# Full-width key and query projections, spread to head rows by DMA, in a gated two-attention kernel

## The chip, the cores and the metric

The kernel runs on one core of one Trainium2 chip. The metric is device time in microseconds (us) of one execution. The core has five engines: TensorE (PE, with its weight loads as PEld), VectorE (DVE), ScalarE (ACT), GpSimd (POOL) and SyncE (SP), which here issues nearly all DMAs. Each engine runs its own instructions in program order; the order between engines comes from semaphores.

## The reference, cut to what matters

```python
g = sigmoid((x * gate_w).sum(-1, keepdims=True))          # x: 1 x 2048 x 512, bf16
# A: full softmax attention, 32 heads of 16
qkv = (x @ A_wqkv).reshape(B, S, 3, 32, 16).transpose(2, 0, 3, 1, 4)
p = softmax(einsum("bhqd,bhkd->bhqk", q, k) * 16 ** -0.5)
a = heads_to_columns(einsum("bhqk,bhkd->bhqd", p, v)) @ A_wo
# B: the same shapes, but a query sees only 8 keys: its own row and every second row before it
idx = pos[:, None] - 2 * arange(8)[None, :]               # masked where negative
b = heads_to_columns(windowed_attention(x @ B_wqkv, idx)) @ B_wo
return g * a + (1 - g) * b
```

## The kernel before

**A planner writes the program.** The class `Sched` simulates the five engines while the kernel is built. Every piece of work is an `Op` with an engine, a duration, dependencies, a due time and the buffers it takes and gives back (`Slots`: two general PSUM buffers "m", two PSUM score rings "rA" and "rB" of 3 and 2 banks, one accumulator "acc", and SBUF buffers). The planner picks, engine by engine, the piece that can start soonest and is due first; that order becomes the program order. Its durations and start times are numbers in the code, such as `S_.t["DVE"] = 2500.0` for the time at which VectorE is taken to be free. On the chip only the order remains, with semaphores.

**Attention A.** The 32 heads are handled as 8 groups of 4; the 2048 queries as 4 chunks of 512 (`QW`), the keys as 16 tiles of 128. One group with one query chunk is a period; there are 32 periods. A unit of work is one head, one key tile and one query chunk: a 128 x 512 block of scores. A period has 64 units, the kernel 2048. In `kt_all` each group's 4 heads sit at partitions 0, 32, 64, 96 with 16 rows of keys each; row 16 of each is a row of ones. The query tile `qt` has the same layout with 16 rows of queries, and row 16 holds minus an upper bound of the scores, so that one 32-row matmul gives score minus bound. Each unit's exponential is made in one of two ways:

- on ACT: PE writes 3 or 2 units into a ring, ACT takes exp of the whole ring (`pT<-ring`, 128x1536 or 128x1024), and PE multiplies with the values (`acc<-pT,vp_all`);
- on DVE, in "quads" of 4 units (`make_quad`): four conversions from PSUM (`dt<-m_ps`), two further terms made in SBUF (`dt<-dt`, 128x2048), and 12 matmuls (`acc<-dt,...`). The planner starts a quad when it sees VectorE free (`d_source`, `start_quad`).

**Projections.** `k_proj` makes one group's keys for 512 positions: four zeroing matmuls (`mm_init`, which also write the row of ones), then 16 matmuls of only 16 columns each, one per head and 128-row slice of the input, each in its own 32-column tile of the array; VectorE copies the result into `kt_all` and takes the largest magnitude (`kmax_all`). `selk` builds a small matrix from it. `q_proj` does the same for queries, takes magnitudes (`absq`), multiplies them with that matrix to fold in the bound (`bound`), and copies out `qt`. `v_proj` projects values with 128-column weights. For the first group the keys are copied by ACT (`first=True`). Each next pair of groups is prepared while the present pair's 8 periods run (`hooks`).

**Attention B.** `b_tile` handles 128 rows at a time, 16 tiles. PE projects, the keys and values go through DRAM (`kv_scr`) and come back shifted 8 times (`ksh`, `vsh`). POOL does nearly all arithmetic in order: 8 products with the query, sums (`prod<-prod`) to logits `lg`, then (`lg<-lg,mx`) the subtraction of the maximum; ACT takes the exponential (`lg<-lg`), VectorE the sum; POOL normalises (`lg<-lg,rr`), multiplies 8 values, adds, and writes `obb`. `final` mixes both attentions for 128 rows and writes them out; the last rows need the last `obb`.

**Keeping PE busy.** `zero_pass` inserts matmuls with zero weights where the planner sees PE's recent activity fall.

Of the kernel before, what the change touches and what calls it, by code (L numbers as in the profile page):

```python
# [36 lines left out]
def _mean_log_ratio():  # L37
    n = 4096
    acc = 0.0
    for k in range(n):  # L40
        y = 128.0 * k / n
        s = 0.0
        for o, w in zip(OFFS, WTS):
# [15 lines left out]
          ("ACT", "DVE"): 1000.0, ("DVE", "POOL"): 800.0, ("SP", "POOL"): 1500.0, ("POOL", "ACT"): 1000.0}  # L59
# [58 lines left out]
class Sched:  # L118
# [31 lines left out]
    def pe_run(self, mms, start, state=None, count=False):  # L150
# [5 lines left out]
        for m, tile_, cols in mms:  # L156
            if m != mode:
                if state is None and count:
                    self.switches += 1
                t = max(t, max(busy) + (SWITCH if "r" in (m, mode) else 0.0))  # L160
                mode = m
            ks = range(4) if tile_ is None else (tile_,)
            t = max(t, max(busy[k] for k in ks))
            if first is None:
                first = t
            if count:
                self.streamed.append((t, t + cols / 2.4, 1.0 if tile_ is None else 0.25))
            for k in ks:
                busy[k] = t + cols / 2.4 + 2.5
            last = t + 174.0 + cols / 2.4  # L170
            t += 15.0
# [112 lines left out]
    def warm(self, ready, op):  # L284

        mms = [("f", None, QW)]
# [45 lines left out]
def kernel(  # L332
# [71 lines left out]
    KEPT = 11  # L404
    for name_, n_ in (("m", 2), ("rA", 1), ("rB", 1), ("acc", 1), ("pTA", 3), ("pTB", 3), ("qt", 3), 
                      ("dt", 8), ("accT", 2), ("ott", 2), ("ksv", 2), ("prod", 1), ("lg", 2),
                      ("kvs", 1), ("qb", 1), ("osb", 3), ("keep", KEPT + 16), ("fb", 1)):
        S_.slots[name_] = Slots(n_)
# [15 lines left out]
    e32 = const.tile([128, 32], BF16, name="e32")  # L424
    V.memset(e32[:], 0.0)
    V.memset(e32[0:1, DH:DH + 1], 1.0)
    selq = const.tile([128, 128], BF16, name="selq")
    V.memset(selq[:], 0.0)
    for j in range(4):
        V.memset(selq[32 * j:32 * j + DH, 32 * j + DH:32 * j + DH + 1], 1.0)  # L430
    ident = const.tile([128, 128], BF16, name="ident")
    make_identity(nc, ident[:])

# [9 lines left out]
    kmax_all = const.tile([128, NG, NC], FP32, name="kmax_all")  # L443
    kmax = const.tile([128, NG], FP32, name="kmax")
    selk_all = const.tile([128, NG, 128], BF16, name="selk_all")
# [5 lines left out]
    S_.t["POOL"] = 9000.0  # L451
    S_.t["DVE"] = 2500.0
# [23 lines left out]
    for name, o, lo in (("wk0", wkv[:, :, 0:G1], D), ("wq0", wq[:, :, 0:G1], 0), ("wv0", wkv[:, :, D:D + G1], 2 * D)):  # L476
        with nc.allow_non_contiguous_dma(reason="columns of one head group"):
            A.dma_start(out=o, in_=a_w3[:, :, lo:lo + G1])
        ld[name] = S_.add(Op("SP", lambda: None, dur=1.0, due=-10.0, lat=4500.0, name=f"ld_{name}"))
    load("x0", x_load(0), 8100.0)  # L480
# [37 lines left out]
    kt_ops = {}  # L518

    def k_proj(i, sc, due, first=False):  # L520
        hold = Hold("m")
        st = {}

        def part(c0, c1):
            def s():
                if c0 == 0:
                    st["pk"] = misc_ps(hold, [128, QW])
                    mm_init(st["pk"], e32, QW)
                pk = st["pk"]
                for c in range(c0, c1):  # L530
                    for j in range(4):
                        h = 4 * i + j
                        mm(pk[32 * j:32 * j + DH, :], wkv[:, c, h * DH:(h + 1) * DH],
                           xT[:, c, sc * QW:(sc + 1) * QW], False, c == DC - 1, tile_position=(0, 32 * j))
            return s

        def evac():
            o = kt_all[:, i, sc * QW:(sc + 1) * QW]
            if first:
                A.copy(out=o, in_=st["pk"][:])  # L540
            else:
                V.tensor_copy(out=o, in_=st["pk"][:])

        def red():
            src = st["pk"][:] if first else kt_all[:, i, sc * QW:(sc + 1) * QW]
            V.tensor_reduce(out=kmax_all[:, i, sc:sc + 1], in_=src, axis=AX.X, op=ALU.max, apply_absolute_value=True)
        slow = 2 if first and sc == 0 else 1
        p1 = Op("PE", part(0, 2), mms=COL4 * (3 * slow), deps=xt_ops[sc] + [ld["wk0" if i == 0 else "wk"]], due=due, acq=[hold], not_before=0.0 if first else due - 5000.0,
                name="k1")
        p2 = Op("PE", part(2, DC), mms=COL4 * (2 * slow), deps=[p1], due=due, name="k2")  # L550
        for o in (p1, p2):
            S_.add(o)
        if first:
            r = S_.add(Op("DVE", red, dur=700.0, deps=[p2], due=due, name="kred"))
            e = S_.add(Op("ACT", evac, dur=650.0, deps=[p2, r], due=due, rel=[hold], name="kev"))
        else:
            e = S_.add(Op("DVE", evac, dur=683.0, deps=[p2], allow=400.0, rel=[hold], name="kev"))
            r = S_.add(Op("DVE", red, dur=677.0, deps=[e], allow=1500.0, name="kred"))
        kt_ops.setdefault(i, []).append(e)
        return r  # L560

    selk_ops = {}

    def selk(i, reds, due):
        def s():
            V.tensor_reduce(out=kmax[:, i:i + 1], in_=kmax_all[:, i, :], axis=AX.X, op=ALU.max)
            V.tensor_scalar(out=selk_all[:, i, :], in0=selq[:], scalar1=kmax[:, i:i + 1], scalar2=-1.02,
                            op0=ALU.mult, op1=ALU.mult)
        selk_ops[i] = S_.add(Op("DVE", s, dur=446.0, deps=reds, due=due, lock=True, name="selk"))
# [3 lines left out]
    def v_proj(h0, h1, tb, TB, due):  # L573
# [4 lines left out]
        def mk(half):  # L578
            def s():
# [3 lines left out]
                for tt in range(lo, hi):  # L583
                    t = tb + tt
                    for c in range(DC):
                        mm(st["pv"][:, tt, :], xT[:, c, t * 128:(t + 1) * 128],
                           wkv[:, c, D + h0 * DH:D + h1 * DH], c == 0, c == DC - 1)
            return s

        def evac():  # L590
# [3 lines left out]
        ops = [Op("PE", mk(0), mms=[("f", None, max(n, 140))] * per, due=due, acq=[hold], not_before=due - 5000.0 if h0 else 0.0,  # L594
                  begun=[] if h0 else [qb_ops[(0, 0)]], name="v1")]
        if TB > 1:
            ops.append(Op("PE", mk(1), mms=[("f", None, max(n, 140))] * per, due=due, name="v2"))
# [19 lines left out]
    qt_ops, qb_ops = {}, {}  # L617

    def q_proj(c_, i, due):
        hold, hq, ha = Hold("m" if (c_, i) != (0, 0) else "acc"), Hold("qt"), Hold("accT")  # L620
        st = {}

        def part(c0, c1):
            def s():
                if c0 == 0:
                    st["p1"] = misc_ps(hold, [128, QW]) if hold.res == "m" else ps.tile([128, QW], FP32, tag="acc", bufs=1, name="p1")
                    mm_init(st["p1"], z32, QW)
                for c in range(c0, c1):
                    for j in range(4):
                        h = 4 * i + j  # L630
                        mm(st["p1"][32 * j:32 * j + DH, :], wq[:, c, h * DH:(h + 1) * DH],
                           xT[:, c, c_ * QW:(c_ + 1) * QW], False, c == DC - 1, tile_position=(0, 32 * j))
            return s

        def absq():
            a = sb(ha, [128, QW], I32, "absq")
            V.tensor_scalar(out=a[:], in0=st["p1"][:].bitcast(I32), scalar1=0x7FFFFFFF, scalar2=None, op0=ALU.bitwise_and)
            st["absq"] = a

        def bound():  # L640
            hi = st["absq"][:].bitcast(BF16).rearrange("p (n two) -> p n two", two=2)[:, :, 1]
            mm_ct(st["p1"], selk_all[:, i, :], hi, False, True, skip_group_check=True)

        def evac():
            qt = sb(hq, [128, QW], BF16, "qt")
            V.tensor_copy(out=qt[:], in_=st["p1"][:])
            qt_tiles[(c_, i)] = qt
        ops = [Op("PE", part(0, 2), mms=COL4 * 3, deps=xt_ops[c_] + [ld["wq0" if i == 0 else "wq"]], due=due, acq=[hold, hq, ha], begun=selk_ops[i].deps if (c_, i) != (0, 0) else [],
                  name="q1"),
               Op("PE", part(2, DC), mms=COL4 * 2, due=due, name="q2"),  # L650
               Op("DVE", absq, dur=683.0, allow=300.0, name="qabs"),
               Op("PE", bound, mms=COL4, due=due, rel=[ha], deps=[selk_ops[i]], name="qb"),
               Op("DVE", evac, dur=683.0, allow=300.0, rel=[hold], name="qev")]
        S_.chain(ops)
        qt_ops[(c_, i)] = (ops[-1], hq)
        qb_ops[(c_, i)] = ops[3]
# [4 lines left out]
    def g_jobs(due):  # L661
# [3 lines left out]
        def zmm():  # L665
            st["zp"] = misc_ps(hz, [128, NT])
            for t in range(NT):
                for c in range(DC):
                    mm(st["zp"][:, t:t + 1], xT[:, c, t * 128:(t + 1) * 128], gw[:, c:c + 1], c == 0, c == DC - 1)
# [5 lines left out]
        def zfin():  # L675
# [4 lines left out]
        ops = [Op("PE", zmm, mms=[("f", None, 70)] * 64, due=due, deps=[o for v in xt_ops.values() for o in v] + [ld["gw"]],  # L680
                  acq=[hz], name="z"),
# [492 lines left out]
    def emit_fill(us, res, n, op):  # L1174
        ring = ps.tile([128, n, QW], FP32, tag=res, bufs=1, name="ring")
        for _ in range(op.zeros):
            mm(ring[:, 0, :], zw[:], ones_t[:], True, True)
# [132 lines left out]
    def make_quad(p, t, late):  # L1310
# [7 lines left out]
        for j in range(4):  # L1318
# [3 lines left out]
            def fill(j=j, hold=hold, st=st):  # L1322
                f_ = fops[j]
                st["s"] = misc_ps(hold, [128, QW])
                for _ in range(f_.zeros):
                    mm(st["s"][:], zw[:], ones_t[:], True, True)
# [151 lines left out]
```

## Time and profile before

| what | value |
|---|---|
| time, median of 3 runs | 800.84 us (797.55 to 804.08) |
| the profiled execution's own time | 798.02 us |
| its span, first to last instruction | 796.0 us |
| busy: PE / DVE / ACT / POOL | 738.2 / 676.4 / 756.2 / 695.4 us |
| mean granted TensorE clock | 0.992 |
| exponentials on ACT: 3-unit / 2-unit, mean | x329, 1530 ns / x328, 1103 ns |
| first exponential of attention A begins | 18.47 us |
| first product of attention B on POOL begins | 56.70 us |
| last `obb` on POOL begins | 787.31 us, lasts 1.27 us |

The span is the stretch between the first and last instruction; about 2 us of the execution lie outside it. Nearly every instruction is recorded at one helper line (L382), so rows are told apart by their tiles: `pT<-ring` reads tile `ring` and writes `pT`. A busy engine need not be the bound: what counts is what its successors wait for.

### The profile page before, as it was taken

The page shows a single profiled execution, that of the slowest core. Times are in us where ns is not written, and L with a number is a line of the kernel's source. Part 1 is how long each engine was busy: PE and PEld are TensorE (multiplying, and loading weights), DVE is VectorE, ACT ScalarE, POOL GpSimd, SP SyncE. Part 2 cuts the span into 40 slices and gives each one's busy share as a digit, 9 for nine tenths or more (in the row PEclk, how much of TensorE's full clock was granted, in tenths as well). Part 3 has the DMA queues.
Part 4 walks back from the last instruction along what each step waited for, and adds up shares of the span by engine and source line. Part 5 has one row for each costly group of instructions (what it writes and reads, how often), then busy time and mean ns, then how long its engine had stood idle before and what let it go on. Part 6 is the DMA issues. An engine that isn't in the chain of part 4 may idle for free.

```text
span 796.0 us, 20219 instructions
## 1 busy us (share of the span) xinstructions
PE 738.2 (93%) x8481; PEld 237.4 (30%) x8481; DVE 676.4 (85%) x1013; ACT 756.2 (95%) x680; POOL 695.4 (87%) x599
## 2 busy tenths in 40 slices
PE   7999999999999989999989899999999989999996
PEld 2332222333232223333322222333222222222222
DVE  3369899888989998989997888978998898888985
ACT  2899999899999999999999999999999999999993
POOL 1019799999999999999899999999998999999896
PEclk9799999999999999999999999999999999999999
DMA  9220321032011212111111121101122210122100
GB/s 206 88 68 12 109 67 55 18 104 68 22 47 54 68 54 68 55 50 42 45 68 54 54 67 54 65 18 55 56 67 81 68 54 30 53 68 67 61 15 34
DMA packets 52074, 47.46 MB, mean 60 GB/s; under 512 B 12048, under 2 KB 49424, under 8 KB 51984
## 3 DMA queue, kind: packets, MB, share of 16 engines
q1 hardware_dynamic: 50400, 45.98, 18.6%
q8 instruction: 66, 1.08, 0.6%
q10 hardware_dynamic: 1584, 0.20, 0.2%
q14 instruction: 24, 0.20, 0.1%
HBM read 37.75 MB, written 6.32 MB: 55 GB/s over the span
## 4 chain that ended last, share of the span: by engine, by line
ACT 29%; PE 28%; DVE 16%; POOL 16%; issue 9%; SPq 1%; DMA 0%; POOLq 0%; DVEq 0%; ACTq 0%
ACT pT L382 29%; POOL prod L382 13%; PE m_ps L382 13%; DVE dt L382 11%; PE acc L382 8%; PE ring L382 7%; SPq L382 1%; POOL lg L382 1%; DVE accT L382 1%; POOL obb L382 1%; POOL ott L382 0%; DVE kt_all L382 0%; DMA xT<-in_A_x_dram 0%; DVE kvs L382 0%; DVE vd_all L382 0%
## 5 line engine op out<-in xcount | busy, mean ns | idle before, releaser
L382 ACT ACTIVATE pT<-ring 128x1536 bf16<-128x1536 f32 (+1 forms) x658 | 750.1, 1316 | 13.2 <-PE ring L382 11.8
L382 PE MATMUL ring<-qt,kt_all 32*128 32x512 bf16 x1644 | 278.0, 383 | 31.0 <-ACT pT L382 25.3
L382 POOL TENSOR_TENSOR prod<-prod 128x512 f32<-128x512 f32 x224 | 295.2, 1324 | 10.8
L382 DVE TENSOR_SCALAR dt<-m_ps 128x512 uint16<-128x512 f32 x404 | 265.3, 676 | 26.8 <-PE m_ps L382 17.5
L382 DVE TENSOR_SCALAR dt<-dt 128x2048 uint16<-128x2048 uint16 x202 | 224.5, 1116 | 1.6 <-PE acc L382 1.0
L382 PEld LDWEIGHTS <-kt_all 32*128 32x128 bf16 (+1 forms) x2304 | 98.1, 91 | 293.1 <-issue 280.8
L382 POOL TENSOR_TENSOR prod<-ksh,qb 128x512 f32<-128x512 bf16 x128 | 161.7, 1292 | 5.6 <-DMA ksh<-kv_scr 3.3
L382 PE MATMUL acc<-pT,vp_all 128*17 128x512 bf16 x1644 | 158.1, 384 | 0.0
L382 POOL TENSOR_TENSOR prod<-vsh,lg 128x512 f32<-128x512 bf16 x128 | 152.2, 1208 | 3.5
L382 PE MATMUL m_ps<-qt,kt_all 32*128 32x512 bf16 x404 | 135.6, 381 | 5.8 <-DVE dt L382 4.5
L382 POOL TENSOR_TENSOR ott<-accT,rden 128x256 bf16<-128x256 f32 x31 | 25.0, 807 | 60.9 <-DVE rden L382 60.8
L382 PEld LDWEIGHTS <-vp_all 128*17 128x17 bf16 x2048 | 46.0, 88 | 107.4 <-issue 99.2
L382 PE MATMUL acc<-dt,vd_all 128*17 128x512 bf16 x808 | 61.1, 379 | 0.0
L382 PE MATMUL m_ps<-bw,xT 128*32 128x512 bf16 x768 | 55.6, 382 | 3.2 <-DVE dt L382 2.0
L382 PE MATMUL acc<-ones_t,zw 128*32 128x512 bf16 (+1 forms) x235 | 51.2, 391 | 1.3 <-DVE accT L382 1.2
L382 PEld LDWEIGHTS <-xT 128*32 128x32 bf16 (+1 forms) x1152 | 32.5, 97 | 32.9 <-issue 26.5
L382 PE MATMUL acc<-dt,vp_all 128*17 128x512 bf16 x404 | 39.6, 383 | 0.0
L382 PE MATMUL m_ps<-xT,wkv 128*16 128x512 bf16 x512 | 38.3, 388 | 1.2 <-DMA xT<-in_A_x_dram 1.2
L382 PE MATMUL m_ps<-xT,wq 128*16 128x512 bf16 x496 | 36.0, 380 | 0.0
L382 DVE TENSOR_SCALAR absq<-m_ps 128x512 int32<-128x512 int32 x31 | 21.3, 686 | 14.7 <-PE m_ps L382 14.4
L382 DVE CAST kt_all<-m_ps 128x512 bf16<-128x512 f32 x28 | 19.2, 687 | 13.3 <-PE m_ps L382 13.0
L382 PEld LDWEIGHTS <-zw 128*32 128x32 bf16 (+1 forms) x367 | 16.7, 94 | 42.7 <-issue 40.8
(72 smaller groups left out, 450.5 us busy)
## 6 DMA issues: line engine op xcount, KB each, us to landing
ksh<-kv_scr SPq DMA_DIRECT2D x16, 1024.0 KB, 5.5
vsh<-kv_scr SPq DMA_DIRECT2D x16, 1024.0 KB, 5.5
kv_scr<-kvs SPq DMA_DIRECT2D x16, 256.0 KB, 2.0
out_dram<-osb SPq DMA_DIRECT2D x16, 128.0 KB, 1.7
bw<-in_B_wqkv_dram SPq DMA_DIRECT2D x1, 1536.0 KB, 9.9
wkv<-in_A_wqkv_dram SPq DMA_DIRECT2D x2, 448.0 KB, 4.9
bwo<-in_B_wo_dram SPq DMA_DIRECT2D x1, 512.0 KB, 3.7
woarr<-in_A_wo_dram SPq DMA_DIRECT2D x8, 64.0 KB, 2.2
```

Of the source, the lines that this page charges most:

```text
L382: return chain_on(key, f(*a, **k))
```

## The change

Keys and queries are projected for two groups (eight heads) at once. `pair_proj` runs four 32-column tiles over the 128 columns of eight heads, without zeroing matmuls. `pair_k` copies the 128x512 result to a buffer `kr`, takes its largest magnitudes, and 8 DMAs of 16x512 spread it into the head rows of `kt_all`. `pair_q` copies to `qr`, makes the magnitudes there and scales them by minus the bound (`kbnd`), sends queries and bound rows to a DRAM tile (`scr`) with two DMAs and fetches each group's query tile with one more. The bound now occupies 16 rows beside each head's 16 query rows, and 16 rows of ones in `kt_all` face them. These ones are written once, at the start, by 7 memsets on VectorE for groups 1 to 7. Group 0 is done differently (`k_first`, `q_first`): VectorE first writes each head's columns of the weights twice side by side (`dup`, into `wd0`), the projection then fills all 32 rows, and small per-row factors (`isq`, `isk`, `isb`, `sgn`, made from the identity matrix) turn the second half into ones or bounds. `selk`, `absq` and the bound's matmuls are gone. The value projection and the zero passes use four 32-column tiles instead of one full-width matmul. The planner's tables are adapted: the buffers (`qt` 4 instead of 3, new `kr` 2 and `qr` 1, `KEPT` 8 instead of 11), margins for SP, a charge for every change of array mode, and the time at which VectorE is taken to be free at the start.

```diff
-    KEPT = 11
+    KEPT = 8
...
-                t = max(t, max(busy) + (SWITCH if "r" in (m, mode) else 0.0))
+                t = max(t, max(busy) + SWITCH)
...
+    r16 = ident[:].rearrange("p (a two d) -> p two a d", two=2, d=DH)
+    V.tensor_reduce(out=isq[:], in_=r16[:, 0], axis=AX.XY, op=ALU.max)
...
     G.memset(vp_all[:, :, :, DH:DH + 1], 1.0)
-    S_.t["POOL"] = 9000.0
-    S_.t["DVE"] = 2500.0
+    for g in range(1, NG):
+        V.memset(kt_all[:, g, :], 1.0)
+    S_.t["DVE"] = 7000.0
...
+    def dup(k, src):
+        for two in range(2):
+            V.tensor_copy(out=wd0[:, k, :, :, two, :], in_=src[:, :, 0:G1].rearrange("p c (h d) -> p c h d", d=DH))
+    for k, name, src in ((0, "wk0", wkv), (1, "wq0", wq)):
+        ld[name + "d"] = S_.add(Op("DVE", lambda k=k, src=src: dup(k, src), dur=420.0, deps=[ld[name]], due=-10.0, lock=True, name="dup"))
...
+    def heads_proj(out, k, sc, c0, c1):
+        for c in range(c0, c1):
+            for j in range(4):
+                mm(out[32 * j:32 * j + 32, :], wd0[:, k, c, j].rearrange("p two d -> p (two d)"), xT[:, c, sc * QW:(sc + 1) * QW],
+                   c == 0, c == DC - 1, tile_position=(0, 32 * j))
...
+    def pair_proj(w2, m, sc, due, hold, acq, deps, name):
...
+                for c in range(c0, c1):
+                    mm_ct(st["p"], w2[:, c, 128 * m:128 * m + 128], xT[:, c, sc * QW:(sc + 1) * QW], c == 0, c == DC - 1)
...
+    def pair_k(w2, m, n, dues, dst, deps, acq, name, groups=(0, 1)):
...
+            def spread(sc=sc, st=st):
+                for e in groups:
                     for j in range(4):
+                        SP.dma_start(out=dst(e)[32 * j:32 * j + DH, sc * QW:(sc + 1) * QW], in_=st["r"][64 * e + DH * j:64 * e + DH * j + DH, :])
...
+    def pair_q(w2, m, sc, n, due, deps, acq, tiles, name, groups=(0, 1)):
...
+            st["r"] = sb(hr, [128, 2, QW], BF16, "qr")
+            V.tensor_copy(out=st["r"][:, 0, :], in_=st["p"][:])
+        def mag():
+            q_, a_ = st["r"][:, 0, :].bitcast(I32), st["r"][:, 1, :].bitcast(I32)
+            V.tensor_scalar(out=a_, in0=q_, scalar1=0x7FFF7FFF, scalar2=None, op0=ALU.bitwise_and)
+            V.tensor_scalar(out=st["r"][:, 1, :], in0=st["r"][:, 1, :], scalar1=kbnd[:, n:n + 1], scalar2=None, op0=ALU.mult)
+        def put():
+            for two in range(2):
+                r = scr[0, 16 * two:16 * two + 1, :]
+                SP.dma_start(out=_ap(r, [[32 * QW, 8], [QW, DH], [1, QW]]), in_=st["r"][:, two, :])
+        def get():
+            for h, e in zip(acq, groups):
+                t_ = sb(h, [128, QW], BF16, h.res)
+                SP.dma_start(out=t_[:], in_=scr[e])
...
     def v_proj(h0, h1, tb, TB, due):
...
-                        mm(st["pv"][:, tt, :], xT[:, c, t * 128:(t + 1) * 128],
-                           wkv[:, c, D + h0 * DH:D + h1 * DH], c == 0, c == DC - 1)
+                        mm_ct(st["pv"][:, tt, :], xT[:, c, t * 128:(t + 1) * 128],
+                              wkv[:, c, D + h0 * DH:D + h1 * DH], c == 0, c == DC - 1)
...
     def zero_pass(now):
...
-        mm(acc_tiles[periods[p]][:], zw[:], ones_t[:], False, False)
+        mm_ct(acc_tiles[periods[p]], zw, ones_t[:], False, False)
...
     def hooks(p):
...
-            k_due(2 * m + 2, now + 0.5 * TPER, 4.0 * TPER)
+            k_due(m + 1, now + 0.5 * TPER, 5.0 * TPER)
-            k_due(2 * m + 3, now + 3.0 * TPER, 4.0 * TPER)
-        if p + 2 < NP:
-            q_proj(periods[p + 2][0], periods[p + 2][1], now + 0.6 * TPER)
+        if p % 2 == 0 and p + 2 < NP:
+            q_pair(periods[p + 2][0], periods[p + 2][1] // 2, now + 0.8 * TPER)
```

## The prediction

> **What bounds the kernel now.** I read the page first (busy shares), then the windows, then the ends of ACT and POOL in the timeline.
>
> ```profile
> PE 738.2 (93%) x8481; PEld 237.4 (30%) x8481; DVE 676.4 (85%) x1013; ACT 756.2 (95%) x680; POOL 695.4 (87%) x599
> ACT 29%; PE 28%; DVE 16%; POOL 16%; issue 9%; SPq 1%; DMA 0%; POOLq 0%; DVEq 0%; ACTq 0%
> ```
>
> No engine owns the chain of work that ended last. The windows show why: two engines are full, but POOL starts late, so that its 87% hides a saturated engine.
>
> ```profile
> 18.00:56.00 38.00, 36.18 (x454) 13.50 (x453) 17.81 (x32) 34.86 (x31) 0.62 (x1) 0.87 0.27 93
> 56.00:751.00 695.00, 652.27 (x7435) 207.68 (x7431) 620.08 (x919) 685.68 (x616) 655.94 (x561) 1.00 0.18 56
> ```
>
> Columns: length, then busy us (and instructions) of PE, PEld, DVE, ACT, POOL, then clock, DMA share, GB/s. From 56 us on ACT is 98.7% busy and POOL 94.4%; the rest of POOL is mostly the gaps between 561 dependent instructions.
>
> ```profile
> 18.47 4.68 ACT L382 ACTIVATE pT<-ring 128x1536 bf16<-128x1536 f32 x4 [1.56 <-PE ring L382]
> ...
> 752.75 0.43 ACT L382 ACTIVATE lg<-lg 128x256 f32<-128x256 f32 x1
> 753.05 29.99 ACT L382 ACTIVATE pT<-ring 128x1024 bf16<-128x1024 f32 x27
> ```
> ```profile
> 56.70 4.94 POOL L382 TENSOR_TENSOR prod<-ksh,qb 128x512 f32<-128x512 bf16 x4 [1.06 <-DMA ksh<-kv_scr]
> ...
> 751.17 1.01 POOL L382 TENSOR_TENSOR lg<-lg,mx 128x256 f32<-128x256 f32 x1 [2.21 <-DVE mx L382]
> ...
> 787.31 1.27 POOL L382 TENSOR_TENSOR obb<-prod 128x512 bf16<-128x512 f32 x1
> ```
>
> ACT ends at 783.04, POOL at 788.58, the span at 796.0: the last rows wait for the last `obb`, and 7.4 us of projection and output follow. So both engines bound the kernel, POOL by a little. POOL needs 731.9 us from its first product (56.70) to its end; ACT needs 764.6 us from its first exponential.
>
> **ACT's pace.** In the chain of waits:
>
> ```profile
> 172.90 1.27 ACT pT L382
> ...
> 175.14 1.09 ACT pT L382
> ...
> 177.37 1.12 ACT pT L382
> ```
>
> One pair of exponentials (5 units) takes 2.235 us, 0.447 us a unit. The 1644 units on ACT are 734.9 us; 16 exponentials of `lg` at 0.43 are 6.9; 22.8 us are lost.
>
> **What the Trainium skill says.**
> - "VectorE: DVE Perf Modes", section "Zero memsets can be issued as uint32 (trn2)": a memset takes one cycle per element whatever the type. The trace agrees that the type doesn't matter: 59 ns for 1 bf16 element, 72 for 16 uint32, 112 for 64 uint32, 485 for 512 bf16, a line of 59 ns plus 0.83 ns per element.
>
> ```profile
> 0.91 0.48 DVE L382 MEMSET ones_t<- 128x512 bf16 x1 [0.91 <-PEq L1462]
> ```
> - "SBUF — State Buffer", section "Who interferes with whom": a VectorE instruction in a 2-port mode (`tensor_scalar` within SBUF) and a GpSimd instruction exclude each other for their whole length. The trace agrees; the columns are minimum/median/maximum ns:
>
> ```profile
> L382 DVE TENSOR_SCALAR dt<-dt x202: 622/1052/1815, 55.5 to 772.2; 128x2048 uint16<-128x2048 uint16 x101
> ...
> L382 POOL TENSOR_TENSOR prod<-ksh,qb x128: 1143/1158/1617, 56.7 to 737.1; 128x512 f32<-128x512 bf16 x128
> ```
> - "TensorE: Matmul & The Clock Gate", section "What's actually happening": PE's clock is halved after some 3.4 us of idleness. The trace shows a granted clock of 0.54 between 20 and 30 us.
>
> **The change, part by part.** Counts are from the order of both programs.
>
> *PE.* Gone are 64 zeroing passes (256 column matmuls), 108 of 256 key and query passes and 32 bound passes: 204 passes of 0.216 us (the spacing of four column tiles in the trace), 44 us. Added are 48 zero passes (159 instead of 111), 10 us, and value matmuls in four times the number (1280 instead of 320). PE waits for ACT already (31.0 us before the ring matmuls), so this gives nothing by itself.
>
> *DVE, steady part.* Gone: 28 key copies (687 ns), 32 `absq` (686), 31 query copies (680), 28 maxima (678), `selk` (4 us): about 85 us. Added: 16 `kr` copies, 16 maxima, 16 `qr` copies at 0.68 us, 33 us; 32 short SBUF operations, between 0.2 us each (as 272 elements of `vd_all` take at least 220 ns) and 0.65 with a wait for POOL; I take 0.45, 14 us. The 38 us freed go straight into 9 more quads: `dt<-m_ps` 404 to 440, `dt<-dt` 202 to 220, which cost 9 x (4 x 0.676 + 2 x 1.116) = 44 us.
>
> *ACT.* 36 units fewer: 36 x 0.447 = 16.1 us. This is what the change brings.
>
> *POOL.* The same instructions. Its excess over the minima of its forms sums to about 76 us; 202 `dt<-dt` and some 20 others cause it, 0.34 to 0.38 us each. Eighteen more cost 6.5 us. The 32 short operations hold the ports for less: 0 to 5 us, I take 1.5; eight `selk` less, -1. POOL: +7 (5 to 12).
>
> *SP.* 112 spreads, 32 puts and 31 gets, at 0.34 to 0.45 us of issue (`woarr`: 3.63 us for 8), 70 us of a queue that mostly waits; a put and a get land in about 2 us each (`kv_scr<-kvs` 2.0, `woarr` 2.2). POOL's loads `ksh` and `vsh` are queued behind them, but are issued some 20 us ahead of use (700.72 for 722.5), so I take nothing; late loads would cost their delay less 20 us. The first query pair is tightest: matmuls at unit 35 of ACT, wanted near unit 56, 9.4 us later, for some 7 us of copy, put and get. Cost 0 to 5 us, once; I take 0.
>
> *At nothing:* `KEPT`, the four-part gate matmul and `kbnd` (under 2 us on a VectorE with gaps); the spread of values over column tiles has the 31 us of PE's waits as cover.
>
> *The start.* Before, the first key matmul runs at 8.58 us and the first exponential at 18.47. Now VectorE must first wait for the identity matrix from POOL (3.24), do four small operations (0.6, estimated from the 0.15 us of `kmax`), seven memsets of 2048 elements, and one `dup` pair (0.45), before PE can begin on keys. A memset is 1.76 us by the trace's line, 2.13 by the skill's cycle (estimate, 0.96 GHz); I take 1.9, 13.4 us for seven. The planner assumes VectorE free at 7.0. Keys start at 3.24 + 0.6 + 13.4 + 0.45 = 17.7, 9.1 us late (8 to 11). PE, idle since 8 us, starts cold: passes of 0.43 us. In program order the first ring now stands behind all key passes, the query pass and all 256 value matmuls of the first group; before, it stood behind 16 of 64. Working through it: keys 0 and 1 and queries to 23.3; half the first value block (64 at 0.027 to 0.033 us, the pace of 48 such in 1.57) to 25.2; keys 2, the other half, the copy, to 28.5; keys 3, then 128 value matmuls, 3.8, to 32.3. First exponential at 32.7: +14.2 us (9 to 18).
>
> *The end.* In the order of ACT the last `lg` exponential, which stood before the last 66 units, now stands behind all 1608. So POOL's remaining chain follows ACT's end. From 751.17 it took 37.4 us. Counted from the exponential: if POOL is left waiting for it, the sum on VectorE (1.1) and the 28.6 us from 759.97 on, less 2.7 for contention and one `ott`, 27 us; if POOL paces itself, two products, two sums and two products more, less the time in which the exponential runs, 32.
>
> **The sum.** By POOL: its first product moves with the start (14.2) and by 5 units of ACT (the B projections stand behind unit 55 instead of 50), 2.2: 73.1. Plus 731.9 + 7 gives 812.0, plus 7.4: span 819.4. By ACT: 32.7 + 1608 x 0.447 + 6.9 + 22.8 = 781.2; plus 27 to 32, plus 7.4: 815.6 to 820.6. Both chains agree. Span 819; with the 2.0 us outside it, 821 us, against the profiled 798.02. The median of the runs before is 2.8 us above that execution and their spread 6.5, so one per cent (8 us) is about what a measurement can tell from no change.
>
> **Rivals.**
> 1. *The start is cheap.* If memsets ran four elements per cycle (0.6 us), VectorE would be ready near 8.5 and the first exponential near 24 (+5.5): by POOL 796 + 5.5 + 2.2 + 7 + 2 = 813; with nothing lost on POOL, 806. For it: the planner's 7.0. Against it: 485 ns for 512 elements.
> 2. *PE's relief reaches ACT (the faster side).* The mechanism is ACT's lost time: 22.8 us, of which 11.8 are waits for the ring. If PE's 34 us less work removed all of it, ACT would end at 32.7 + 718.8 + 6.9 = 758.4 and the kernel at 758.4 + 27 + 7.4 + 2 = 795. It decides from the point where POOL has the last logits ready by then, 20 us before its own sum allows. Against it: in the long window ACT idles only 9.3 of 695 us, and the new start brings new waits.
> 3. *The spread by DMA stalls periods.* A query pair later than its period stops the ring. With 28 us of slack in steady state only the first is at risk; if all 15 others lost 1 us, 836.
> 4. *The granted clock falls*, since column tiles replace full zero passes: 3% of the span, 24 us, at half clock would stretch by up to half, 12 us: 833. The planner counts a set of four column tiles like one full pass, and column tiles fed most of the 0.992 before.
>
> **How the numbers follow.** My forecast 0.72 (808 to 832), rival 1 0.12, rival 2 0.05, rivals 3 and 4 together 0.11. Predicted 821. The range reaches down to rival 1 without POOL's loss (806, and 2 of spread) and up past rival 4, and leaves out rival 2 and the far end of 3: 804 to 834. Faster by over 1%: rival 2 with rival 1's start as well, 787, 0.04. Within 1%: the rest of rival 2, the lower part of rival 1 and the forecast's own low edge, 0.12. Slower: 0.84.
>
> **What would show it.** Right: seven memset rows of 1.7 to 2.2 us, first key matmul after 16 us, first `pT` after 28; `pT` with 1608 units and ACT idle for the last 30 us while POOL works; `dt<-dt` 220 times. Wrong: memset rows near 0.6 us; POOL's 732 us shrinking; a clock under 0.97 after 40 us; long waits of the ring for `qt`.

## The result, and the profile after

The changed kernel takes 827.4 us (median of 4 runs, 825.97 to 828.95) where the kernel before takes 800.7 (median of 4): a ratio of 1.0333, 95% interval 1.0284 to 1.0382. It is slower, as forecast; 821 was predicted. The profiled execution took 825.97 us with a span of 824.2. Ratios, here and below, leave out executions that fell into a slower state of the chip, so that a ratio can lie below the quotient of two medians.

The busy times and the chain of work that ended last:

```profile
PE 715.3 (87%) x9222; PEld 231.4 (28%) x9222; DVE 703.0 (85%) x1036; ACT 740.4 (90%) x665; POOL 697.9 (85%) x599
ACT 34%; DVE 23%; PE 21%; issue 12%; POOL 8%; DMA 1%; POOLq 0%; DVEq 0%; ACTq 0%; SPq 0%
```

PE does 23 us less and ACT 16 us less than before, as planned, VectorE 27 us more, and the span is 28 us longer. Shares don't say where those 28 us lie. The starts in the timeline do (start, busy us, engine, line, operation, idle time before it):

```profile
4.18 1.76 DVE L382 MEMSET kt_all<- 128x2048 bf16 x1 [0.38 <-issue]
...
19.05 1.04 PE L382 MATMUL m_ps<-xT,accT 128*32 128x512 bf16 x8 [10.68 <-DVE accT L382]
...
32.18 10.49 ACT L382 ACTIVATE pT<-ring 128x1536 bf16<-128x1536 f32 x9 [1.96 <-PE ring L382]
...
783.12 0.48 ACT L382 ACTIVATE lg<-lg 128x256 f32<-128x256 f32 x1
```
```profile
70.08 5.40 POOL L382 TENSOR_TENSOR prod<-ksh,qb 128x512 f32<-128x512 bf16 x4 [5.03 <-DMA ksh<-kv_scr]
...
813.80 1.26 POOL L382 TENSOR_TENSOR obb<-prod 128x512 bf16<-128x512 f32 x1
```

PE stands idle for 10.68 us until VectorE has done seven memsets (the second starts at 6.32, so each takes 2.14 us) and doubled the weights. At the other end ACT is done at 783.60, and GpSimd works on alone until 815.06. Two ledgers, both worked out from these starts, give the same 28.2 us:

| stretch (us) | before | after | difference |
|---|---|---|---|
| start to first exponential of A | 18.47 | 32.18 | +13.7 |
| first exponential to ACT's end | 764.6 | 751.4 | -13.2 |
| ACT's end to the span's end | 13.0 | 40.6 | +27.6 |
| start to GpSimd's first product | 56.70 | 70.08 | +13.4 |
| first product to GpSimd's end | 731.9 | 745.0 | +13.1 |
| GpSimd's end to the span's end | 7.4 | 9.1 | +1.7 |

ACT did get shorter by the change's 16 us less 3. What it gained was given back at both ends: at the start, where everything waits for VectorE, and at the end, where only GpSimd works.

Two more things are new. The granted clock of PE was 1.00 in every stretch of the kernel before from 56 to 751 us. After, five drops stand in it, in each of which it falls to 0.50 for some us; these are the first two, in windows of 5 us (length, then busy us of PE, PEld, DVE, ACT, POOL, then clock, DMA share, GB/s):

```profile
140.00:145.00 5.00, 4.92 (x68) 2.13 (x67) 4.62 (x6) 4.63 (x6) 4.76 (x5) 0.55 0.48 126
210.00:215.00 5.00, 3.92 (x32) 0.72 (x30) 4.41 (x8) 3.56 (x4) 4.69 (x5) 0.72 0.47 137
```

No single wait of PE in the 20 us ahead of any of the five was longer than 1.19 us. What set them off is not shown.

And the short operations on `qr` are not short (min/median/max ns, first and last start):

```profile
L382 DVE TENSOR_SCALAR qr<-qr x16: 223/642/1351, 47.8 to 724.5; 128x256 int32<-128x256 int32 x16
L382 DVE TENSOR_SCALAR qr<-qr,kbnd x16: 353/1124/1325, 48.2 to 725.4; 128x512 bf16<-128x512 bf16 x16
```

### The profile page after: what moved, and what is told of

It reads as the page before. It is cut to its first block, busy times and chain, and to the rows that moved or that the text cites. A ratio compares the mean times of both kernels' runs of the same rounds, so it can differ in the third digit from the quotient of the medians.

```text
span 824.2 us, 21995 instructions
## 1 busy us (share of the span) xinstructions
PE 715.3 (87%) x9222; PEld 231.4 (28%) x9222; DVE 703.0 (85%) x1036; ACT 740.4 (90%) x665; POOL 697.9 (85%) x599
## 4 chain that ended last, share of the span: by engine, by line
ACT 34%; DVE 23%; PE 21%; issue 12%; POOL 8%; DMA 1%; POOLq 0%; DVEq 0%; ACTq 0%; SPq 0%
ACT pT L382 33%; DVE dt L382 16%; PE m_ps L382 8%; PE acc L382 7%; POOL prod L382 7%; PE ring L382 5%; DVE kt_all L382 2%; DVE qr L382 1%; DVE accT L382 1%; DVE kvs L382 1%; DMA qt<-q_scr 1%; POOL lg L382 0%; ACT lg L382 0%; DVE vp_all L382 0%; DVE vd_all L382 0%
## 5 line engine op out<-in xcount | busy, mean ns | idle before, releaser
L382 ACT ACTIVATE pT<-ring 128x1536 bf16<-128x1536 f32 (+1 forms) x643 | 734.7, 1321 | 16.6 <-PE ring L382 14.1
L382 DVE TENSOR_SCALAR dt<-m_ps 128x512 uint16<-128x512 f32 x440 | 287.9, 677 | 37.4 <-PE m_ps L382 24.7
L382 PE MATMUL ring<-qt,kt_all 32*128 32x512 bf16 x1608 | 269.9, 386 | 40.2 <-ACT pT L382 35.5
L382 DVE TENSOR_SCALAR dt<-dt 128x2048 uint16<-128x2048 uint16 x220 | 240.0, 1099 | 0.4
L382 PE MATMUL m_ps<-qt,kt_all 32*128 32x512 bf16 x440 | 148.8, 385 | 12.2 <-DVE dt L382 8.3
L382 POOL TENSOR_TENSOR ott<-accT,rden 128x256 bf16<-128x256 f32 x31 | 23.6, 761 | 78.9 <-DVE rden L382 78.8
L382 PE MATMUL acc<-ones_t,zw 128*32 128x512 bf16 x712 | 67.5, 395 | 1.4 <-DVE accT L382 1.2
L382 PEld LDWEIGHTS <-zw 128*32 128x32 bf16 x764 | 19.8, 95 | 50.8 <-issue 48.5
L382 PEld LDWEIGHTS <-vd_all 128*17 128x17 bf16 x880 | 22.4, 91 | 20.4 <-issue 2.3
L382 DVE CAST kvs<-m_ps 128x512 bf16<-128x512 f32 x32 | 21.7, 679 | 6.6 <-PE m_ps L382 6.6
L382 DVE STREAM_TRANSPOSE accT<-acc 128x512 f32<-128x512 f32 x32 | 22.6, 707 | 3.2 <-PE acc L382 2.8
```

The source lines that it names most:

```text
L382: return chain_on(key, f(*a, **k))
```

## The experiments

The theory: the start moves every later event, one for one; and behind the change GpSimd's chain sets the end, with ACT's 16 us idle behind it. The rivals: the loss sits in the steady part (column tiles and clock, the spread by SyncE, VectorE's load). Each ratio is against the kernel before, run beside it; the changed kernel's own is 1.0333.

### Dose and response at the start: fewer and more memset cycles

The same bytes as half as many elements:

```diff
-        V.memset(kt_all[:, g, :], 1.0)
+        V.memset(kt_all[:, g, :].bitcast(FP32), 1.0 + 0x3F80 / 2.0 ** 23)
```

> The seven memsets stay where they are, but each writes the same bytes as 1024 elements of 32 bits instead of 2048 of 16. Theory: a memset costs per element whatever its size, so start to start falls from 2.14 to about 1.07 us, the first key matmul comes at 11.6 instead of 19.05, the first exponential at about 24.5, and the time falls by 7.5 us to about 820 (817 to 823). Rival (the start does not carry through to the end): 825 to 829. Rival (cost goes with bytes): rows and time as in the changed kernel.

Measured: 823.2 us, ratio 1.0296 (1.0242 to 1.0349). The second memset starts at 5.04, so they follow each other at 1.07 us instead of 2.14: the cost goes by elements and not by bytes.

```profile
3.97 0.91 DVE L382 MEMSET kt_all<- 128x1024 f32 x1 [0.16 <-issue]
```

The first key matmul came at 11.59, the first exponential at 26.1 (6.1 earlier), the end 4.2 earlier: by the medians somewhat less than the 7.5 expected.

All seven twice:

```diff
     for g in range(1, NG):
         V.memset(kt_all[:, g, :], 1.0)
+    for g in range(1, NG):
+        V.memset(kt_all[:, g, :], 1.0)
```

> The seven memsets are issued twice in a row, nothing else changes; the second seven are dead work. Theory: fourteen of 2.14 us, first key matmul at 34.0, first exponential at about 47, time up by 15 us to about 842 (840 to 845). Rival (the start has slack behind it that another engine sets): up by clearly less than 15.

Measured: 844.0 us, ratio 1.0553 (1.0507 to 1.0599). First key matmul at 34.0, first exponential at 46.5, the end 16.6 us later. From 26.1 over 32.2 to 46.5 us for the first exponential, the stretch from it to ACT's last stayed at 751 to 754 us and the part behind ACT's end at 40.6: between the two runs the first exponential moves by 20.4 us and the end by 20.8. So the start goes through to the end; on either side of the changed kernel alone that holds to some 2 us (4.2 for 6.1, and 16.6 for 14.3).

### The memsets later: a miss that shows another mechanism

```diff
-    for g in range(1, NG):
-        V.memset(kt_all[:, g, :], 1.0)
...
                 st["r"] = sb(hr, [128, QW], BF16, "kr")
                 V.tensor_copy(out=st["r"][:], in_=st["p"][:])
+                if sc == 0:
+                    for e in groups:
+                        V.memset(kt_all[:, 2 * m + e, :], 1.0)
```

> The seven memsets of ones are taken out of the start; each group's memset is issued on VectorE just before the first spread of that group (one memset early in the first period, two for each later pair), everything else in the same order. Theory (the late start shifts both ACT and POOL through to the end): the first key matmul moves from 19.05 to about 8.6-9 us, the first exponential from 32.2 to about 21.5, POOL's first product from 70.1 to about 59.6, and the time falls by the same 10.5 us, from 827.4 to about 817 (814 to 820). Rival (the loss sits in the steady part: column tiles, clock, SyncE): the start moves, the end does not; 824 or more.

Measured: 846.1 us, ratio 1.0562 (1.0494 to 1.0631): 19 us slower than the changed kernel, although its keys started at 8.2 us and its first exponential at 23.6. Neither theory has room for that. The timeline around the first pair of deferred memsets shows what happens, the first of two memsets on VectorE, then PE, then ACT, then the windows:

```profile
100.48 1.76 DVE L382 MEMSET kt_all<- 128x2048 bf16 x1 [0.38 <-issue]
```
```profile
104.98 0.37 PE L382 MATMUL m_ps<-qt,kt_all 32*128 32x512 bf16 x1 [3.35 <-DVE dt L382]
```
```profile
105.67 1.45 ACT L382 ACTIVATE pT<-ring 128x1536 bf16<-128x1536 f32 x1 [3.40 <-PE ring L382]
```
```profile
100.40:104.70 4.30, 1.24 (x18) 0.30 (x11) 3.85 (x3) 1.88 (x2) 4.30 (x5) 1.00 0.03 8
...
109.00:114.00 5.00, 5.00 (x38) 0.79 (x30) 2.46 (x5) 3.16 (x3) 4.84 (x6) 0.50 0.10 29
```

The two memsets hold VectorE for 4.3 us. PE's next score matmul needs a buffer that VectorE has to empty, and the ring's matmuls stand behind it in PE's program: PE does 1.24 us of work in 4.3. Then the granted clock is 0.50 from about 106 to 119 us (0.63 in the window from 104.7 to 109, 0.50 in the next two, 0.96 from 119 to 124), PE is busy without a gap, and ACT, waiting for the ring, works 3.16 of 5 us. Between 102 and 120 us ACT loses 7.6 us (the eight waits before its exponentials, added): the hold-up of 4.3 us, and most of it again. "TensorE: Matmul & The Clock Gate", section "What's actually happening", in the Trainium skill, has such a case: after an idle window of some 3.4 us the clock is halved until PE has been busy for one such window. Here 3.35 us of waiting were followed by half clock, but for some 13 us, longer than the one busy window that the page names; and the five drops of the changed kernel came after much shorter waits than the page's. Over the whole run ACT's waits for the ring rose to 38.1 us, from 14.1.

### A cheap way to write ones, and full-width values

```diff
-        V.memset(kt_all[:, g, :], 1.0)
+        V.tensor_copy(out=kt_all[:, g, :].rearrange("p (a n) -> p a n", n=QW), in_=_ap(ones_t[:], [list(ones_t[:].ap[0]), [0, S // QW], [1, QW]]))
...
-                        mm_ct(st["pv"][:, tt, :], xT[:, c, t * 128:(t + 1) * 128],
-                              wkv[:, c, D + h0 * DH:D + h1 * DH], c == 0, c == DC - 1)
+                        mm(st["pv"][:, tt, :], xT[:, c, t * 128:(t + 1) * 128],
+                           wkv[:, c, D + h0 * DH:D + h1 * DH], c == 0, c == DC - 1)
```

> The ones of groups 1 to 7 are copied on VectorE from the 512 ones of ones_t (a bf16 copy within SBUF, 2048 elements) instead of set by memset, at the same place; and the value projection is full-width again, so that PE meets 64 instructions instead of 256 ahead of the first ring. Zero passes keep their column tiles; the order is the same. Theory (start carries through, the middle of 751-754 us from the first exponential to the last of lg and the tail of about 41 us stay): a copy of 2048 costs about what dt<-dt costs undisturbed, 0.62 us, so the first key matmul comes near 9 us, the first exponential near 21.5 (no wait of PE inside the value block), and the time falls by 10 to 11 us to about 817 (814 to 820). Rival (the 846 us of the deferred memsets came from the early start itself, and not from VectorE being held for 4.3 us at a time in mid-run): the clock falls in the middle again and the time is 830 or more.

Measured: 815.1 us, ratio 1.0172 (1.0132 to 1.0211). The seven copies together take what two memsets took:

```profile
3.72 4.30 DVE L382 COPY kt_all<-ones_t 128x2048 bf16<-128x2048 bf16 x7
```

The keys start at 8.34 and the first exponential at 18.95, the start of the kernel before. From there to ACT's end it is 753.8 us, the part behind it 40.6: the rest of the changed kernel is untouched. With the memsets kept, but values and zero passes full-width (the next run), the first exponential comes at 30.8 instead of 32.2, so that nearly all of the 13 us at the start is the copies' doing. So the start is 12 us of the 26.7, and the miss of the deferred memsets came from where they were put and not from starting early. Both of these runs differ at the start in one more thing: with deferred memsets (and 256 value matmuls of 32 columns) PE stopped for 5.04 us near the end of the value block, for no reason that the profile names; with 64 full-width ones it did not.

### The column tiles undone

Value projections and all zero passes full-width, with the memsets left as they are: the second part of the edit above, and this one in each zero pass:

```diff
-        mm_ct(acc_tiles[periods[p]], zw, ones_t[:], False, False)
+        mm(acc_tiles[periods[p]][:], zw[:], ones_t[:], False, False)
```

> Only the column tiles are undone: value projections and zero passes are full-width matmuls again (a quarter as many instructions), in the same order. Theory: PE does not bound, so the time stays within 3 us of 827.4; the mean granted clock may rise by 0.01. Rival (the lower granted clock of 0.968 costs the time): the clock comes back to about 0.99 and the time falls by 8 to 12 us.

Measured: 831.9 us, ratio 1.0409 (1.0353 to 1.0464), a clock of 0.963. The clock did not come back and the time did not fall (it rose by 6 us, by the ratios, where the theory allowed 3; the two intervals overlap). Column tiles are not the cause.

### GpSimd relieved onto VectorE, in both kernels

`ott` is the result of a period of attention A: the sums in `accT`, scaled by `rden`, the reciprocals that VectorE makes at the period's end. The scaling moves to VectorE, in the planner's list of work too, so that it writes another order:

```diff
-            (V if last else G).tensor_tensor(out=so["ott"][:, :, half * DH:half * DH + DH], in0=st["accT"][:, :, 0:DH], in1=rd_bc,
+            (V if last or True else G).tensor_tensor(out=so["ott"][:, :, half * DH:half * DH + DH], in0=st["accT"][:, :, 0:DH], in1=rd_bc,
```

In the changed kernel:

> In the changed kernel the 31 scalings of ott that run on GpSimd (23.6 us, and 17 us of waits for rden after the first) go to VectorE; the planner then makes 645 instead of 643 exponentials and 109 instead of 110 quads, and the start is unchanged. Theory (after the change GpSimd is the bound, not ACT): GpSimd's stretch from its first product shrinks from 745 to about 720, the tail behind the last exponential from 40 to about 15-20 us, and the time falls by 16 to 25 us, to 802-811. Rival (ACT's chain sets the end, GpSimd merely follows it): within 4 us of 827.

In the kernel before:

> The same move of the ott scalings to VectorE, in the kernel before. Theory (there ACT's end and GpSimd's lay 5.5 us apart, so that ACT takes over as soon as GpSimd is relieved): the time falls by no more than 5 us, 796 to 801, with GpSimd ending some 20 us ahead of the end. Rival (GpSimd alone bounded the kernel before as well): 780 to 785.

Measured: 844.5 us, ratio 1.0548 (1.0479 to 1.0617), and 842.2 us, ratio 1.0478 (1.0403 to 1.0553). None of the four expectations held. In the changed kernel's variant:

```profile
L382 DVE TENSOR_TENSOR ott<-accT,rden x32: 401/654/1378, 63.8 to 829.0; 128x256 bf16<-128x256 f32 x32
```
```profile
POOL lg L382 <- DVE mx L382: 61.5, 15, 15.2
```

(The second fence is from the waits: us in total, times, longest.) The scaling costs VectorE up to 1378 ns, against 0.41 or 0.42 us in the three cases in which GpSimd stood idle. "SBUF — State Buffer", section "Who interferes with whom", of the skill, states that a VectorE instruction with two SBUF inputs contends with a GpSimd instruction that reads SBUF, which the spread agrees with. What GpSimd was relieved of loaded VectorE; GpSimd waited 61.5 us for the maxima `mx` from VectorE, the clock fell to 0.924, and ACT waited 47.9 us for the ring. The run says nothing on whether GpSimd bounds.

The copies, the full-width values and the scaling on VectorE at once, with attention B started earlier:

```diff
-            b_tile(b_next[0], now + (2000.0 if p > 2 else 22000.0))
+            b_tile(b_next[0], now + (2000.0 if p > 2 else 4000.0))
```

> The copies of ones and the full-width value projection as in the run with copies, the ott scalings on VectorE, and the first tiles of attention B due 4 us instead of 22 us after their period begins. Theory (the freed 36 units of ACT are worth something once neither the start nor GpSimd takes them back): first exponential near 21.5, GpSimd's first product near 45, ACT's last exponential near 773, a tail of 13-15 us, time about 788 (782 to 797), below both kernels. Rival (the middle of ACT's work stretches when VectorE gets the extra scalings and the clock dips): 800 or more.

Measured: 850.8 us, ratio 1.0506 (1.0453 to 1.056). GpSimd did begin at 41.2 us, but ACT waited 61.8 us for the ring and ended its exponentials after 823. The rival holds.

### GpSimd relieved by leaving work out, in both kernels

```diff
-            padd(ltree(hf, 4, 0, 4), 1260.0)
+            if hf:
+                padd(ltree(hf, 4, 0, 4), 1260.0)
```

In the changed kernel:

> The changed kernel without one of GpSimd's sums: for the first four of the eight shifted keys of each tile of attention B the third sum of products (128x512, 1.26 us) is left out, 16 in all, 20 us of GpSimd's work. Nothing moves to another engine; the planner makes its order anew (the last exponential of lg then stands ahead of the last 39 units of ACT instead of behind all). Theory (after the change GpSimd's chain sets the end): the time falls by nearly all of it, 17 to 22 us, to 805-811, and the tail from the last exponential of lg on is no longer the end of ACT as well. Rival (ACT's chain or the clock sets the end): within 5 us of 827.

In the kernel before:

> The same sum left out in the kernel before (20 us less for GpSimd, the planner's order made anew, the last exponential of lg ahead of the last 122 units). Theory (there ACT's end lay 5.5 us ahead of GpSimd's and takes over at once): 796 to 803, no more than 5 us below 800.7, with GpSimd ending some 15 us before the end. Rival (GpSimd alone bounded the kernel before too): 780 to 785.

Measured: 822.0 us, ratio 1.0237 (1.0143 to 1.033), and 809.0 us, ratio 1.0129 (1.0068 to 1.0191). The theory wanted 20 us off the changed kernel; its ratio fell by one per cent, 8 us, and the two intervals overlap. The control, meant to stay, rose by 10 us by its ratio, although it does less. In the first, GpSimd's busy time fell from 697.9 to 676.2 us, but from first product to end it took 744.8 (745.0 before): the work left out came back as waiting.

```profile
POOL ott L382 <- DVE rden L382: 92.6, 24, 60.4
ACT pT L382 <- PE ring L382: 29.7, 45, 2.4
```

In the changed kernel the same two rows read 78.8 us in 21 waits and 14.1 us in 22. `ott` stands in GpSimd's program at the end of a period of attention A, so GpSimd can't run ahead of ACT and PE. Its last such wait came at 778.22, behind the last logits of attention B: every sum that was left out lay ahead of it, and what was saved on them ended in waits. And leaving an operation out made the planner write another order, in which ACT waits twice as long for the ring. The clock was 0.93 to 0.95 in every 100 us from 100 to 500.

### Fewer quads

```diff
-    LATE = 2000.0
+    LATE = -6000.0
```

> The changed kernel with one number of the planner altered (LATE from 2000 to -6000), which starts a quad only when more time is left: 103 quads instead of 110, so 28 units go back to ACT (+12.5 us of exponentials) and 14 of the port-holding dt<-dt leave VectorE; GpSimd's first product comes some 4 us earlier in the plan. Theory (GpSimd bounds; each dt<-dt costs it 0.36 us): the time falls by 6 to 11 us, to 816-821, although ACT gets more to do. Rival (ACT's units set the end): it rises by about 12 us, to 840.

Measured: 828.5 us, ratio 1.0297 (1.0198 to 1.0396), between the two theories and no different from the changed kernel. ACT's 28 more units cost what fewer `dt<-dt` and the earlier first product (66.0) saved, or a worse order hides both; this run can't part them.

### The tail shared out

With the order of PE, ACT and VectorE left as it was up to the last exponential, the end alone is changed, on top of the run with copies. For the last two tiles of attention B the eight weighted values are added up by PE; the last tile's weights and products run on VectorE:

```diff
+                if t >= PE_FROM:
+                    for w_ in range(W):
+                        mm(st["ptp"][:, c, :], late_prod(t, w_)[:, c * 128:(c + 1) * 128], ident[:], w_ == 0, w_ == W - 1)
...
-            G.tensor_tensor(out=st["lg"][:], in0=st["lg"][:], in1=over_w(st["rr"]), op=ALU.mult)
+            (V if t >= DVE_FROM else G).tensor_tensor(out=st["lg"][:], in0=st["lg"][:], in1=over_w(st["rr"]), op=ALU.mult)
```

Here `PE_FROM` is tile 14, `DVE_FROM` tile 15, and `late_prod` a place for the bf16 products in the part of `xT` that is no longer read.

> The run with copies (ones copied by VectorE, full-width value projection), with the same order of PE, ACT and VectorE up to the last exponential, and another end: for the last two tiles of attention B the sums of the eight weighted values are made on PE (32 accumulating 128x128 matmuls with the identity in place of 16 transposes of obb), and the last tile's normalisation and eight products run on VectorE, which is idle there, instead of GpSimd. Theory (with the order fixed, the end is ACT's last exponential plus a tail of 41 us of serial work that no other engine shares): first and last exponentials as in the run with copies (18.9 and about 772 us), the tail falls from 41 to about 21 us, and the time from 815 to about 795 (790 to 801), level with the kernel before or up to 1% below it. Rival (the tail is bound by PE's cold passes and the waits between engines, not by GpSimd's work): 805 or more.

Measured: 800.1 us over 22 runs beside 800.3 for the kernel before, ratio 0.9997 (0.9975 to 1.0018): 15 us off the run with copies.

```profile
776.35 0.48 ACT L382 ACTIVATE lg<-lg 128x256 f32<-128x256 f32 x1
```
```profile
790.40 2.17 PE L382 MATMUL m_ps<-ident,xT 128*128 128x128 bf16 x32 [0.86 <-DVE kt_all L382]
```

From the last exponential of `lg` to the span's end (799.7) it is 23.4 us instead of 41.1. PE makes the last tile's sums, transposed at once, in 2.17 us; a single sum of 128x512 takes GpSimd 1.26.

## Why the prediction was right, and where it was not

**The start.** Predicted +14.2 us, measured +13.7. The copies brought all of it back. Inside the step two errors met: the memset was taken at 1.9 us between the trace's line and the skill's cycle, and is 2.14 from start to start, which is the one cycle per element that "VectorE: DVE Perf Modes", section "Zero memsets can be issued as uint32 (trn2)", states (2.13, an estimate in the prediction); the value block was faster than assumed (64 matmuls in 0.71 us), with an unexplained stop of 1.7 us behind it. That they met so closely is luck. The slow passes of 0.43 us came as forecast, from 19.05 us to 24.5, though the record of the granted clock reads 1.00 there; from 25.0 us on four such passes took 1.06 us together instead of 1.82.

**ACT.** Predicted end 781.2, measured 783.6. The 36 units were saved; lost time was 24.6 us (751.4 less 1608 x 0.447 and 8.0 for `lg`) for 22.8 assumed.

**GpSimd's stretch.** The sign was right, the term was mis-sized and its mechanism only partly right. Predicted +7 us by contention, measured +13.1, of which busy time is 2.5. The rest is waiting: for `rden` 17.6 us after the first wait (78.8 less 61.2), before it was 9.0 (60.8 less 51.8); for `mx` 10.0, before 6.6. The prediction had no term for such waits. It put the 39 us in which GpSimd idles between 56 and 751 us in the kernel before mostly to gaps between instructions, but 19 of them were waits already (9.0 and 6.6 as above, 2.2 for `ksh`, 1.2 for `rr`). Why they grew is not shown: ACT as a whole was not slower, so the order, or the local drops of the clock, is left.

**The `qr` operations.** Assumed 0.45 us each, measured 0.66 (mean of `qr<-qr`) and 0.93: 25.5 us on VectorE instead of 14. At 207 us two of them, 0.75 and 1.12 us, stand ahead of the copies that PE waits for, and the drop of the clock to 0.72 follows. That they caused it was not tried; with the deferred memsets such a drop followed when VectorE was held for 4.3 us.

**The clock (rival 4).** Given small weight, and half right: the mean is 0.968. More than half of what is missing lies behind ACT's end, at 0.65, where PE has little to do. It is not from column tiles, as the full-width run shows. And the 0.54 of the kernel before, which the prediction set beside the skill's 3.4 us of idleness, followed waits of PE of 1.27 us at most. Where the clock is low ACT loses time: with less of GpSimd's work, ACT was busy 93 to 96% in the four 100-us windows at 0.93 to 0.95, and 98.7% in the next, at 1.00.

**The tail.** From the last exponential to GpSimd's end 31.5 us, predicted 27 to 32; it is the prediction's second branch, in which GpSimd paces itself, as the lines below show. After it 9.1 us, predicted 7.4: PE's clock was 0.64 in the last 24 us. Of the 41 us, 17.7 could be shared out.

**What fell.** "So both engines bound the kernel, POOL by a little" is not borne out for the changed kernel as a whole. With 20 us of GpSimd's work left out, the time fell by 8 us and GpSimd's stretch not at all. What the runs support is that the written order binds the two together, through `ott` in GpSimd's program and `lg` in ACT's. Only the end is GpSimd's alone. These are its last wait in the changed kernel, and its first use of what follows from ACT's last exponential:

```profile
718.55 0.94 POOL L382 TENSOR_TENSOR ott<-accT,rden 128x256 bf16<-128x256 f32 x1 [1.20 <-DVE rden L382]
...
788.67 0.63 POOL L382 TENSOR_TENSOR lg<-lg,rr 128x256 f32<-128x256 f32 x1
```

From 718.55 to 815.06 GpSimd works without a wait. Even ACT's last exponential doesn't hold it up: VectorE has `rr` ready at 786.42. So 31.5 of the 40.6 us behind ACT's end are the rest of 96 us of GpSimd's own work. Work taken from GpSimd at the close of this stretch shortened the kernel (15 us, the shared tail); work taken from ahead of its last wait did not. Whether GpSimd would bind in an equally good order stays open: each edit that made the planner write a new order also cost waits for the ring (from 18.5 us, with fewer quads, to 61.8, for 14.1), in the kernel before too (809 us with less work).

**The spread by DMA (rival 3).** PE's matmuls waited 1.1 us in all for `qt`'s transfers, so it was hidden, as assumed. **PE's relief (rival 2)** did not reach ACT: waits for the ring were 14.1 us, before 11.8.

The sum came to a span of 819 against 824.2: 3 us too late in GpSimd's first product (73.1 for 70.08), 6 too few in its stretch, 2 too few behind it. That the errors partly cancel is luck; the sign, the late start and the long tail are not.

## What to carry to other kernels

Setting up constants on an engine that the first useful work waits for costs its full length at the end; look for the form that the engine does fast, since here a copy of ones took 0.61 us where a memset took 2.14. Freeing a full engine is worth something only if the last dependent chain is shortened as well: here 16 us less for ACT turned into a longer stretch in which one engine worked alone, and sharing out that tail gained 15. Where engines run in a written order, an engine with idle time can still be unable to take 2 to 4 us at once: VectorE at 85% had gaps, but holding it for 4.3 us stopped PE, half clock followed, and ACT lost 7.6. And before work is taken off an engine, ask whether the engine waits for something behind that work: if it does, the gain can come back as waiting.

## What the runs showed of the hardware

- A bf16 memset of 2048 elements on VectorE reads 1765 ns in its row and takes 2.14 us from start to start; as 1024 elements of 32 bits it takes 1.07. An idle time of 0.38 or 0.16 us stands before each of the seven, so the row alone shows too little.
- After PE stood still for 3.35 us its granted clock was 0.50 for about 13 us, though it was busy throughout. In five other places it fell to 0.50 with no wait of PE above 1.19 us in the 20 us before.
- 64 matmuls of 64 columns in four column tiles passed in 0.71 us and 16 full-width ones in 0.64, or 0.04 each; one after the other 64 would be 2.6. So the four tiles ran side by side even at this size.
- VectorE's two-input scaling of 128x256 took 0.41 to 0.43 us in the eight cases, in the two runs with it moved, in which GpSimd stood idle; over all cases its median was 654 ns and its longest 1378 in the changed kernel's variant, where GpSimd was mostly at work.
